# Attention in chunks and a gated feed-forward: another way to bring in v, and another start

## The chip, the cores and the metric

The kernel runs on one core of a Trainium2 chip. The metric is the device time of one execution in microseconds (us). The kernel before took 248.11 us, the median of three runs (247.49 to 249.26).

A core has engines that each work through their own instructions in order and meet at semaphores: TensorE (PE) multiplies matrices, VectorE (DVE) and ScalarE (ACT) do elementwise work, GpSimd (POOL) and SyncE (SP) are used here mostly to issue DMAs (transfers). A tile in SBUF or PSUM has up to 128 partitions, written first in a shape such as 128x512.

## The reference

There are q, k and v of 4 batches, 8 heads, 768 tokens and 64 channels, and 8 memory keys and values for each batch and head. Queries attend in chunks of 32:

```python
for c in range(nc):                      # 24 chunks
    l_start = max(0, 32 * c - 16)        # 16 tokens of left context
    r_end = min(S, 32 * c + 32 + 8)      # 8 tokens of right context
    k_full = np.concatenate([mem_k, k[:, :, l_start:r_end]], axis=2)
    v_full = np.concatenate([mem_v, v[:, :, l_start:r_end]], axis=2)
    scores = scale * np.matmul(q_c, k_full.transpose(0, 1, 3, 2))
    a = softmax(scores)                  # maximum taken off, sum + 1e-9
    out[:, :, c_start:c_end] = np.matmul(a, v_full)
```

The result, as 3072 tokens of 512 channels x, goes through a gated feed-forward with 1536 hidden channels:

```python
gate = np.maximum(x @ w_gate, 0.0)
val = x @ w_val
return (gate * val @ w_out).astype(np.float32)
```

Everything comes and goes as float32. The kernel multiplies in 2-byte types.

## The kernel before, in words

**Tiles.** A tile is 128 tokens of one batch, four chunks, all eight heads: 24 tiles, six for each batch. Each chunk sees 64 keys: 16 left, 32 own, 8 right, 8 memory. The feed-forward works on blocks of 2, 2, 2, 4, 4, 4, 4 and 2 tiles (`BLOCKS`). For each block and each of 12 parts m of 128 hidden channels there are two groups of four matmuls, gate (`g_ps`) and val (`v_ps`, line 396), a relu on ACT (line 402) and a product on DVE (line 408). Then `out_ps` (line 421) is made from w_out, copied by ACT and stored. The gate and val weights come in four groups of parts, 0 to 1, 2 to 5, 6 to 8 and 9 to 11 (`GROUPS`), and the first two blocks take turns by these groups.

**A tile's chain.** The transposes of q and k (`qk_ps`), their copies to `qT` and `kT`, the scores (PE, `s_ps`, line 298), the row maximum (DVE, `mx`, line 311), the difference (DVE, `dif`, line 318), the exponents (ACT, three instructions, line 326, which also reorder the 64 keys to own, right, memory, left), the sum (DVE, line 330), the reciprocal, the product with it (`p_n`, line 341), the transpose (`pT`, line 347), a copy, the values (`xT_ps`), and a copy to `xT`, the feed-forward's input.

**v.** Batches 1 to 3 are loaded into `v_bd`, two tiles of block-diagonal weights. In each, the even heads' 64 key slots lie in partitions 0 to 63 and the odd heads' in partitions 64 to 127; one holds chunks' left, own and right rows (56), then 8 memory rows. Each chunk's 56 rows are read from DRAM (line 173), so that a token that two or three chunks see is read more than once. POOL fills the tile with zeros ahead of its first use (line 129). The values of one tile are then 16 matmuls (line 377). Batch 0 goes another way: v is loaded by tiles of 128 tokens in their natural order (`v_n`, line 188), and PE moves the rows to their chunk slots by multiplying with shifted identities cut from `band` (`vs_ps`, line 204). ACT or DVE copy the result to `v_q`. Its values take 4 matmuls for the memory rows (line 363) and 32 small ones (line 370).

**q and k.** Batch 0 is loaded in pairs of tiles (`qk_p`, line 216), two neighbouring tokens in a partition, and transposed in 8 matmuls for each tile (line 225). The others are loaded tile by tile (`qk_b`, line 243); from tile 18 on SP's DMA transposes them. POOL's loads convert float32 to 2-byte types on the way.

**Order.** Nothing is ordered by hand. `schedule` plays the kernel through with a cost and a priority for each operation and gives every engine the ready operation of the highest priority; the order found is the order in the program, and the engines keep it, whatever the real times are. Loads on POOL keep the order in which they are listed; at most eight are in flight. That list begins with the first k and q pairs, `band`, the second k pair, three `v_n`, weight group 0, the second q pair, the third k pair, two `v_n`, and the weight groups 1 to 3.

Of the kernel before, what the change touches and what calls it, by code (L numbers as in the profile page):

```python
# [9 lines left out]
F32 = mybir.dt.float32  # L10
# [9 lines left out]
def kernel(  # L20
# [20 lines left out]
    CH = 32  # L41
# [11 lines left out]
    BAND0 = 48  # L53

    LATE_QK, LATE_P = 18, 18

# [25 lines left out]

    band = const.tile([128, BAND0 + 176], F16, name="band")
    ident_h = band[:, BAND0:BAND0 + 128]
# [12 lines left out]
    v_q = v_bd[0][:, 0:2].rearrange("p h c d -> p (h c d)").rearrange("p (h c d) -> p h c d", h=HP, d=D)  # L97
    v_n = {}
    qk_p = {(i, r): const.tile([128, H, 2 * D], BF16, name=f"qk_p_{i}_{r}") for i in range(2) for r in range(TPB // 2)}
# [15 lines left out]
    def make_band():  # L115
        nc.gpsimd.memset(band, 0.0)
        nc.gpsimd.affine_select(
            out=band, in_=band, compare_op=ALU.not_equal, fill=1.0, base=BAND0,
            pattern=[[-1, BAND0 + 176]], channel_multiplier=1)

# [7 lines left out]
    def zero(eng, t, hp):  # L128
        eng.memset(t[:, hp].rearrange("p c d -> p (c d)").bitcast(F32), 0.0)  # L129


    def mem_load():
        for par in range(2):
            nc.sync.dma_start(
                kmem_f[:, par, :],
                bass.AP(tensor=mem_k.tensor, offset=mem_k[0, par, 0, 0].offset,
                        ap=[[2 * NMEM * D, B * HP], [D, NMEM], [1, D]]),
            )
# [13 lines left out]
    def mem_rows(eng, b, n):  # L152
        hp, par = divmod(n, 2)
        p = slice(64 * par + CTX, 64 * par + CTX + NMEM)
        src = vmem[p, b, HP * par + hp]
# [22 lines left out]
    def v_parts(b, par, c0, c1):  # L178
        parts = []
        if (b, par, c1) == (B - 1, 1, HP * NCH):  # L180
            c1 -= 1
            parts.append((b, par, 0, 48, c1, c1 + 1))
        return parts + [(b, par, 0, CTX, c0, c1)]


    def load_v_tile(t):
        v_n[t] = ldpool.tile([128, H, D], F16, tag="qk_b", name="v_n")
        nc.gpsimd.dma_start(
            v_n[t],
            bass.AP(tensor=v.tensor, offset=v[0, 0, 128 * t, 0].offset,  # L190
                    ap=[[D, 128], [S * D, H], [1, D]]))

    def shift(c0):
        ps = TMP["sh", c0] = fps.tile([128, 2, HP, D], F32, tag="fps", name="vs_ps")
        for i in range(2):
            t, g = divmod(c0 + i, 4)
            parts = [(t, BAND0 + CH * g - 16)]
            if g == 0 and t:
                parts.append((t - 1, BAND0 + 112))
            if g == 3 and t < TPB - 1:  # L200
                parts.append((t + 1, BAND0 - 48))
            for n, (src, x) in enumerate(parts):
                for par in range(2):
                    nc.tensor.matmul(ps[D * par:D * par + D, i], lhsT=band[:, x:x + 64],  # L204
                                     rhs=v_n[src][:, HP * par:HP * par + HP, :],
                                     start=(n == 0), stop=(n == len(parts) - 1))

    def shift_copy(c0, eng):
        copy(eng, v_q[:, :, c0:c0 + 2, :].rearrange("p h c d -> p c h d"), TMP.pop(("sh", c0)))

# [37 lines left out]
    def new_batch(b):  # L248
        qT[b] = kvpool.tile([128, HP, S], BF16, name="qT")
        kT[b] = kvpool.tile([128, HP, NCH, KW], BF16, name="kT")  # L250
        src = kmemT[:, b]
        nc.vector.tensor_copy(
            kT[b][:, :, :, 16:16 + NMEM],
            bass.AP(tensor=src.tensor, offset=src.offset,
                    ap=[src.ap[0], [NMEM, HP], [0, NCH], [1, NMEM]]))
# [535 lines left out]
```

## Time and profile before

| | before |
|---|---|
| median of three runs | 248.11 us |
| the profiled execution | 247.81 us |
| its span | 246.0 us |
| PE busy | 233.3 us, 95% |
| DVE busy | 132.7 us, 54% |
| ACT busy | 117.6 us, 48% |
| POOL busy, mostly issuing DMAs | 90.6 us, 37% |
| first gate or val matmul | at 22.24 us |

The span is the time from the first to the last instruction that the profiler saw; the execution's own time has 1.8 us around it. Matmuls overlap, so that the time of a group is better read from the start of one group to that of the next. A row of the timeline gives start, duration, engine, line of the kernel, operation, what is written from what, how many instructions are merged, and in brackets how long the engine had been idle and what ended that. In a row of waits, the engine and what waited stand left of the arrow, what it waited for stands right of it.

### The profile page before, as it was taken

Reading aid. Unit: us, or ns where it says so; the run is one execution under the profiler, and the core shown is the slowest. Engines: PE = TensorE matmul, PEld = TensorE weight load, DVE = VectorE, ACT = ScalarE, POOL = GpSimd, SP = SyncE. Lnnn points to the kernel's source line nnn. Section 1 sums busy time; section 2 is a strip of 40 time slices with the busy share of each in tenths; the row PEclk is TensorE's granted clock in tenths of the full one; section 3 lists DMA queues with packets and bytes.
Section 4 is the critical chain, followed back from the end, with each engine's and each line's share of the span. In section 5 each row is a group of like instructions: output and inputs, shape, how many; then the busy total and the mean of one; then the engine's idle time right before and its main releaser. Section 6 shows DMA issues by size and latency. Waiting matters only on the chain.

```text
span 246.0 us, 6397 instructions
## 1 busy us (share of the span) xinstructions
PE 233.3 (95%) x2673; PEld 139.8 (57%) x2673; DVE 132.7 (54%) x260; ACT 117.6 (48%) x265; POOL 90.6 (37%) x105
## 2 busy tenths in 40 slices
PE   0869999999999999999999999999999999999994
PEld 0646887884488645555445545555445444444873
DVE  2372757984139748796048779999342034320430
ACT  2755867753275445643245575765332232312432
POOL 8965799813268991099921050000000000000000
PEclk9999999999999999999999999999999999999999
DMA  7999999999999899999999999671101210002102
GB/s 74 173 179 203 203 96 119 174 175 127 133 223 154 80 102 136 75 75 147 179 192 158 67 76 109 130 147 25 23 0 45 85 44 0 0 35 95 43 3 85
DMA packets 109757, 25.76 MB, mean 105 GB/s; under 512 B 100769, under 2 KB 106657, under 8 KB 109729
## 3 DMA queue, kind: packets, MB, share of 16 engines
q0 software_dynamic: 94368, 16.42, 107.7%
q1 hardware_dynamic: 11760, 2.64, 8.9%
q10 hardware_dynamic: 3600, 6.29, 7.9%
q8 instruction: 21, 0.34, 0.6%
q14 instruction: 8, 0.06, 0.1%
HBM read 32.06 MB, written 6.29 MB: 156 GB/s over the span
## 4 chain that ended last, share of the span: by engine, by line
PE 92%; DMA 2%; DVE 2%; issue 1%; ACT 1%; POOL 1%; ACTq 0%; POOLq 0%
PE v_ps L396 26%; PE g_ps L396 26%; PE out_ps L421 25%; PE xT_ps L377 3%; PE s_ps L298 3%; PE qk_ps L264 2%; DMA qk_p<-in_k_dram 2%; PE pT_ps L347 2%; PE xT_ps L370 2%; PE vs_ps L204 1%; PE qk_ps L225 1%; PE xT_ps L363 1%; DVE mx L311 1%; POOL qk_p L216 1%; DVE dif L318 1%
## 5 line engine op out<-in xcount | busy, mean ns | idle before, releaser
L408 DVE TENSOR_TENSOR gvT<-v_ps,g_relu 128x256 f16<-128x256 f32 (+1 forms) x96 | 53.0, 555 | 56.7 <-PE v_ps L396 41.0
L396 PE MATMUL g_ps<-xT,w_gate_sb 128*128 128x256 f16 (+1 forms) x384 | 78.5, 327 | 0.0
L396 PE MATMUL v_ps<-xT,w_val_sb 128*128 128x256 f16 (+1 forms) x384 | 78.2, 326 | 0.0
L402 ACT ACTIVATE g_relu<-g_ps 128x256 f16<-128x256 f32 (+1 forms) x96 | 46.9, 489 | 50.7 <-PE g_ps L396 50.0
L421 PE MATMUL out_ps<-w_out_sb,gvT 128*128 128x512 f16 (+2 forms) x300 | 65.7, 371 | 0.0
L396 PEld LDWEIGHTS <-w_gate_sb 128*128 128x128 f16 x384 | 36.4, 98 | 24.0 <-issue 0.4
L396 PEld LDWEIGHTS <-w_val_sb 128*128 128x128 f16 x384 | 35.9, 98 | 20.9 <-issue 0.2
L421 PEld LDWEIGHTS <-gvT 128*128 128x128 f16 x300 | 28.0, 98 | 29.9
L78 ACT COPY o_sb<-out_ps 128x512 f32<-128x512 f32 (+2 forms) x25 | 14.2, 567 | 37.2 <-PE out_ps L421 28.2
L326 ACT ACTIVATE p_exp<-dif 128x256 f16<-128x256 f32 (+2 forms) x72 | 19.5, 336 | 9.0 <-DVE dif L318 8.8
L243 POOL DMA_DIRECT2D qk_b<-in_k_dram x18 | 16.5, 915 | 15.0 <-issue 8.4
L311 DVE TENSOR_REDUCE mx<-s_ps 128x8 f32<-128x512 f32 x24 | 16.5, 688 | 8.3 <-PE s_ps L298 8.0
L156 POOL DMA_DIRECT2D v_bd<-vmem x16 | 10.1, 642 | 27.7 <-DMA v_bd<-in_v_dram 27.7
L330 DVE TENSOR_REDUCE sm<-p_exp 128x8 f32<-128x512 f16 x24 | 16.4, 682 | 6.0 <-ACT p_exp L326 5.9
L78 ACT CAST xT<-xT_ps 128x512 f16<-128x512 f32 x19 | 11.1, 584 | 15.4 <-PE xT_ps L377 10.2
L243 POOL DMA_DIRECT2D qk_b<-in_q_dram x18 | 16.4, 913 | 3.1 <-issue 2.0
L341 DVE TENSOR_TENSOR p_n<-p_exp,rinv 128x512 f16<-128x512 f16 x24 | 16.5, 687 | 0.4
L318 DVE TENSOR_TENSOR dif<-s_ps,mx 128x512 f32<-128x512 f32 x24 | 16.4, 684 | 0.4
L173 POOL DMA_DIRECT2D v_bd<-in_v_dram x7 | 14.0, 2015 | 1.0 <-POOL v_bd L129 0.6
L377 PEld LDWEIGHTS <-v_bd 128*128 128x128 f16 x288 | 9.6, 96 | 4.7 <-issue 1.1
L78 ACT COPY kT<-qk_ps 128x512 bf16<-128x512 bf16 x17 | 10.8, 641 | 2.9 <-PE qk_ps L225 1.9
L129 POOL MEMSET v_bd<- 128x1536 f32 x8 | 10.7, 1397 | 0.0
(52 smaller groups left out, 156.8 us busy)
## 6 DMA issues: line engine op xcount, KB each, us to landing
out_dram<-o_sb ACTq DMA_DIRECT2D x23, 256.0 KB
v_bd<-in_v_dram POOLq DMA_DIRECT2D x5, 672.0 KB, 17.6
qk_b<-in_k_dram POOLq DMA_DIRECT2D x18, 128.0 KB, 6.1
qk_b<-in_q_dram POOLq DMA_DIRECT2D x18, 128.0 KB, 6.4
w_out_sb<-in_moe_w_out_dram POOLq DMA_DIRECT2D x2, 768.0 KB, 11.2
qk_p<-in_k_dram POOLq DMA_DIRECT2D x3, 256.0 KB, 5.2
qk_p<-in_q_dram POOLq DMA_DIRECT2D x3, 256.0 KB, 7.1
v_n<-in_v_dram POOLq DMA_DIRECT2D x6, 128.0 KB, 6.5
```

Of the source, the lines that this page charges most:

```text
L78: nc.scalar.copy(o, i)
L243: nc.gpsimd.dma_start(qk_b[a, i], bass.AP(tensor=x.tensor, offset=x[b, 0, 128 * t, 0].offset, ap=[[D, 128], [S * D, H], [1, D]]))
L311: nc.vector.reduce_max(SM[a, "mx"], s4, axis=AX.X)
L318: nc.vector.tensor_tensor(out=SM[a, "dif"].rearrange("p (m r) a s -> p r m a s", r=2), in0=S_ps.pop(a).rearrange("p r (m a) s -> p r m a s ...
L326: nc.scalar.activation(p[:, :, :, s0:s0 + k1 - k0], dif[:, :, :, k0:k1], ACT.Exp, scale=SCALE)
L330: nc.vector.reduce_sum(SM[a, "sm"], SM[a, "p"], axis=AX.X)
L341: nc.vector.tensor_tensor(out=P_n[a], in0=SM.pop((a, "p")), in1=rinv_b, op=ALU.mult)
L377: nc.tensor.matmul(ps[:, hp, r], lhsT=v_bd[b % NSET][:, hp, 4 * t + g, :], rhs=x[:, hp, r], start=True, stop=True)
L396: nc.tensor.matmul(ps, lhsT=w[:, f, 128 * m:128 * m + 128], rhs=xTs[blk][:, f, :], start=(f == 0), stop=(f == NFC - 1))
L402: nc.scalar.activation(st["r", m], st.pop((0, m)), ACT.Relu)
L408: nc.vector.tensor_tensor(out=st["gv"][:, m, :], in0=st.pop((1, m)), in1=st.pop(("r", m)), op=ALU.mult)
L421: nc.tensor.matmul(st["o", t, c], lhsT=st["gv"][:, m, 128 * t:128 * t + 128], rhs=w_out_sb[:, m, c[0]:c[1]], start=(m == 0), stop=(m == ND ...
```

## The change

- **v.** All batches use `v_bd`. Each token is loaded once, into the 32 lower slots of a chunk; these are the 16 left rows and the first 16 own rows, so the chunk grid of the load is shifted by 16 tokens. The other 24 slots of a chunk are copied inside SBUF from the next chunk's lower slots (`upper`, eight copies for each batch on DVE; `upper_tile` for tiles 0 and 1, by ACT or DVE). Batch 0's v is loaded first on POOL, in two halves for even and odd heads. `v_n`, `band`, the shift matmuls and the extra form of the values go. For batch 0 the zeros in `v_bd` are written in 12 pieces by DVE or ACT, and the memory rows are copied by eight DMAs on SP.
- **The first q and k.** Tiles 0 and 1 are loaded as float32 from the queues of SP and ACT into space that is free at the time, converted by DVE or ACT, and transposed in 4 matmuls each. The first eight keys of tiles 1, 2 and 4, which a neighbour's chunk needs, are loaded on their own (`next_load`).
- **Tile 1's exponents** are taken straight from PSUM, one ACT instruction for each head with the negative maximum as bias and the sum as a second result. The reordering of the keys moves to the product with the reciprocal, now three instructions.
- **PE** multiplies zeros (`idle_product`) where the plan has nothing for it up to its 14th us. The plan's costs change with it, and until its 24th us an engine may wait 0.4 us for an operation of higher priority.

In the order that comes out, PE does the first feed-forward group after the values of tiles 0 and 1 and the transposes of the second k pair; ACT has its `upper_tile` copies from v's first half ahead of tile 0's exponents and one from its second half ahead of tile 1's; POOL issues the identity, v's first half, 16 rows, v's second half, weight group 0, the second k and q pairs, group 1, group 2, the third pairs and group 3, with zero fills of the other `v_bd` between them.

```diff
-    band = const.tile([128, BAND0 + 176], F16, name="band")
+    idle = const.tile([128, 128], BF16, name="idle")
+    HEAD = 2
+    DIRECT = (1,)
+    def zero_other(t, par, e):
+        p, c, d = slice(64 * par, 64 * par + 64), slice(4 * t, 4 * t + 4), slice(D - D * par, 2 * D - D * par)
+        x = v_bd[0][p, :, c, d].bitcast(F32)
+        if e == "DVE":
+            nc.vector.memset(x, 0.0)
+            return
...
+    def idle_product(N):
+        if "idle" not in TMP:
+            TMP["idle"] = fps.tile([128, 512], F32, tag="fps", name="idle_ps")
+        nc.tensor.matmul(TMP["idle"][:, 0:N], lhsT=idle, rhs=idle[:, 0:N], start=True, stop=True)
+    def raw_load(eng, x, a, i):
+        src = (q, k)[i]
+        n = 128 if a < HEAD else NMEM
+        eng.dma_start(
+            qk_f[0:n, x],
+            bass.AP(tensor=src.tensor, offset=src[0, 0, 128 * a, 0].offset,
+                    ap=[[D, n], [S * D, H], [1, D]]))
+    def raw_cast(x, a, i, eng):
+        qk_b[a, i] = ldpool.tile([128, H, D], BF16, tag="qk_b", name="qk_b")
+        copy(eng, qk_b[a, i], qk_f[:, x])
-    def load_v_tile(t):
...
-    def shift(c0):
...
+    def upper(b, par, i0, i1, eng):
+        x = v_bd[b % NSET].rearrange("p h c d -> p (h c) d")
+        d = slice(D * par, D * par + D)
+        copy(eng, x[64 * par + CH:64 * par + CTX, i0:i1, d], x[64 * par:64 * par + CTX - CH, i0 + 1:i1 + 1, d])
+    def upper_tile(par, t, eng):
+        d = slice(D * par, D * par + D)
+        copy(eng, v_bd[0][64 * par + CH:64 * par + CTX, :, 4 * t:4 * t + 4, d],
+             v_bd[0][64 * par:64 * par + CTX - CH, :, 4 * t + 1:4 * t + 5, d])
+    def exponent_direct(a):
+        s, nb = S_ps.pop(a), SM.pop((a, "nb"))
+        p = SM[a, "p"] = smpool.tile([128, HP, 2, 64], F16, name="p_exp")
+        SM[a, "sm"] = smpool.tile([128, HP, 2], F32, name="sm")
+        for hp in range(HP):
+            m, r = divmod(hp, 2)
+            for par in range(2):
+                x = 2 * m + par
+                nc.scalar.activation(p[:, hp, par, :], s[:, r, x, :], ACT.Exp, scale=SCALE, bias=nb[:, r, x:x + 1],
+                                     accum_out=SM[a, "sm"][:, hp, par:par + 1])
...
-        if b == 0:
-            for hp in range(HP):
-                nc.tensor.matmul(ps[:, hp, :], lhsT=vmem_0[:, hp, :], rhs=x[:, hp, :],
-                                 start=(hp == 0), stop=False, skip_group_check=True)
...
+    def load_v_op(b, par, deps):
+        n = HP * NCH
+        load(("vl", b, par), CH * n, CH * n * 1.05e-3,
+             lambda: load_v_rows(b, par, 0, CH, 0 if b or par else 1, n), deps)
...
-    load_pair_op(0, 1)
-    load_pair_op(0, 0)
-    load("ident", 0, 0, make_band)
+    load("ident", 0, 0, make_ident)
+    load_v_op(0, 0, [])
+    load_v_op(0, 1, [])
+    load_w_op(0)
     load_pair_op(1, 1)
-    for t in range(3):
-        load_v_nat(t)
-    load_w_op(0)
     load_pair_op(1, 0)
+    load_w_op(1)
+    load_zero(0)
+    load_w_op(2)
...
+                            alone = len(ops[key]["eng"]) == 1 or e == "ACT"
+                            if e != "PE" and t < HASTE and alone and ready(ops[key], t + 0.4):
+                                break
                         if o is None:
+                            if e == "PE" and 1.3 < t < WARM:
+                                order.append((t, lambda: idle_product(128)))
+                                free[e] = t + (0.107 if t < 5.5 else 0.056)
```

## The prediction

> **What bounds the kernel now.** Read the page from the top. The first view gives the busy time of each engine, the second the same in 40 slices of 6.15 us.
>
> ```profile
> span 246.0 us, 6397 instructions
> ...
> PE 233.3 (95%) x2673; PEld 139.8 (57%) x2673; DVE 132.7 (54%) x260; ACT 117.6 (48%) x265; POOL 90.6 (37%) x105
> ...
> PE   0869999999999999999999999999999999999994
> ```
>
> TensorE (PE) is busy 233.3 of 246.0 us and full from the fourth slice to the last but one. Of the 12.7 us idle, 3.15 lie in the last 4 us (results leave; the change does not touch that) and 0.67 at 67 us. The rest, about 9 us, comes before 18.5 us. So two things can move the time: matmuls taken out of the full stretch, and the moment at which the full stretch begins. The timeline shows that moment.
>
> ```profile
> 22.24 1.03 PE L396 MATMUL g_ps<-xT,w_gate_sb 128*128 128x256 f16 x4
> ...
> 23.55 1.36 PE L204 MATMUL vs_ps<-v_n,band 128*64 128x256 f16 x12
> 24.75 0.39 PE L225 MATMUL qk_ps<-ident_b,qk_p 128*64 128x128 bf16 x8
> 25.07 0.61 PE L396 MATMUL v_ps<-xT,w_val_sb 128*128 128x256 f16 x4
> ```
>
> One feed-forward group (four matmuls) runs at 22.24 us, the next only at 25.07; from there they follow each other every 0.43 us (25.07, 25.52, 25.95). The group at 22.24 took 1.03 us, later ones 0.60; twelve shift matmuls took 1.36 us at 23.55 and 0.85 at 26.72. PE runs at about half speed until 24.6 us, though the granted clock reads 1.00 throughout. I count the full stretch from 24.75 us.
>
> **1. PE work, after 24.75 us.** Gone: 34 of the 68 shift matmuls at 0.071 us (twelve in 0.85): 2.4 us. The values of tiles 2 to 5 took 0.93 us each (31.23 to 32.16); the form that replaces them (L377) takes 0.91 for two tiles (67.74 to 68.65): 4 x 0.48 = 1.9. Coming back, because the changed order does it after its first feed-forward group: 16 transposes of the second q pair (37.79 to 38.36, 0.57), the scores of tile 2 (0.31), one group (0.43): 1.3. Net **-3.0**.
>
> **2. When the feed-forward starts.** In the changed order of ACT the two copies that fill tiles 0 and 1 from v's first half stand ahead of tile 0's exponents, and one that needs v's second half stands ahead of tile 1's. ACT works in order, so everything waits for v. On POOL the identity comes first (0.75 us, 3.14 to 3.89 before), then v: its first issue moves from 1.25 to 2.0 us. In this trace the first pair load was issued at 1.25 and had landed at 6.20, the second at 7.66: 1.46 us per load, so 3.5 us pass before data flow; v flows from 5.5 us. Its two halves are 6,128 runs of 64 elements. The nearest rows are the v_n loads (1,024 such runs each, three of them between 9.12 and 12.42 us, so at most 1.1 us per 1,024) and the later v_bd loads (10,752 runs, about 52 to 67.7 us, 1.5 per 1,024). I take 1.3: landed at 9.4 and 13.3 us. The four float32 loads use the same DMA engines; they start 1.3 us sooner, so I charge one of them, 1.0 us: v's second half at **14.3**. Bounds: 12.1 (1.1, nothing beside it) and 20.3 (1.5, all four in the way at 1.46).
>
> From there ACT does: copy 1.05 (from 0.616 for 512 and 0.265 for 128 elements), eight exponents by head 1.5 (the 64-column form takes 0.241 alone, but three forms of 1.01 together run in 0.81; bounds 1.0 to 1.9), copy 1.05, then pT, a zero fill, pT, xT, a zero fill, xT at 0.58 each: 3.5. That is 7.1, and x of both tiles is ready at **21.5**. The first scores do not end later: k, q and the memory keys are issued at 0.74 instead of 1.25, two casts are added (0.58), and even scores at 9.7 as before leave tile 0's exponents ahead of 14.3. PE is full from 21.5 instead of 24.75: **-3.25**. DVE saves dif and sum of tile 1 (0.68 each), beside that wait and so worth nothing; its added fills and copies also fit there.
>
> The idle products (154 matmuls on zeros) cost nothing where PE waits. The 53 ahead of the first pT cover 3.0 us at 56 ns, and then PE waits again until 18 us. Before, PE ran 3.7 us almost without a gap (20.9 to 24.6) before matmuls got short. The Trainium skill (TensorE: Matmul & The Clock Gate, "What's actually happening") says that a window of about 3.4 us without work halves the clock, and as long a busy one restores it. By that rule the first 3.4 us of feed-forward would still be slow and the sum about 1 us higher; the trace agrees on the busy side (3.7 us).
>
> **3. What is late next.** From 21.5 to the values of tile 3, PE has 48 pair transposes (1.7), 18 groups (7.8), two scores (0.6), two pT (0.6), two values (0.9): 11.6 us. Before, scores 2 to values 3 took 13.2 us (23.21 to 36.4), of which 3.3 lay between the two scores; the new order has one group there (0.75 with the scores). So 10.7, and 2.7 ahead of scores 2: 13.4. PE idles the difference, **+1.8**. Weights: POOL's issues at the end of the queue were released at 23.06, 24.38, 25.64, so 1.3 us per 512-column load. Behind v: group 0 (2.6) 16.9, two pairs 19.8, group 1 24.9, group 2 28.7, two pairs 31.6, group 3 35.4. Needed from about 25 and 29.5: just in time. They stand behind v in one queue and move with it.
>
> **4. Batches 1 to 3.** v's runs fall from 56 to 32 rows per chunk, which removes the 0.67 us at 67 us:
>
> ```profile
> 67.74 1.06 PE L377 MATMUL xT_ps<-pT,v_bd 128*128 128x32 f16 x32 [0.67 <-PE out_ps L421]
> 68.03 0.58 ACT L78 COPY o_sb<-out_ps 128x512 f32<-128x512 f32 x1 [2.93 <-DMA out_dram<-o_sb]
> 68.07 0.88 POOL L243 DMA_DIRECT2D qk_b<-in_k_dram  x1 [5.28 <-DMA v_bd<-in_v_dram]
> ```
>
> POOL's DMA there ended with v, as did PE's wait. Added: 24 DVE copies of 24x1536. The nearest row is the copy of 768 two-byte elements inside SBUF, 0.31 at its best, so 0.62: 15 us on an engine that is 46% idle, in rows of four (2.5 us) ahead of reductions. I put 0.2 us a row for six rows: 1.2. Net **+0.5**. The other end is the same copy beside a v issue:
>
> ```profile
> 84.22 4.40 POOL L173 DMA_DIRECT2D v_bd<-in_v_dram  x2 [0.57 <-POOL v_bd L129]
> ...
> 84.69 1.90 DVE L252 COPY kT<-kmemT 128x768 bf16<-128x768 bf16 x1
> ```
>
> It took 1.90 us, ending as the first issue did. Beside a shorter issue at 37.44 it took 0.35. The Trainium skill (SBUF — State Buffer, "Who interferes with whom") says that such a DVE copy and GpSimd exclude each other for a whole instruction, the later one waiting. By that rule each row of four waits for an issue in progress; what it would cost is rival E.
>
> **Sum.** 246.0 - 3.0 - 3.25 + 1.8 + 0.5 = 242.05 us of span. The profiled execution took 247.81, 1.8 more than its span: **243.9 us**. Against the median of 248.11 that is 1.7% less; 1% (245.6 to 250.6) is about what this kernel's measurement can tell. Every microsecond by which v's second half misses 14.3 counts one to one, since exponents and weights stand behind it.
>
> **Rivals.** A, the forecast, 242 to 246, chance 0.38.
> B, v at its best rate (12.1) and the chain of tiles 2 and 3 hidden: 246 - 3.0 - 5.45 + 0.5 + 1.8 = 239.9. For it: the v_n rows are the nearest in time. Against: eight loads share the DMA engines. 0.20.
> C, the gain of the start is given back: x of tile 3 comes at 36.4 as before, DVE having five fills and eight copies ahead of tile 2's maximum, and PE still slow (+1.2). 246 - 3.0 + 0.5 + 1.2 + 1.8 = 246.5. For it: 4 us of added DVE work there. Against: before, DVE idled 4.56 us ahead of that maximum. 0.16.
> D, slower: v arrives late. It lands in 32 partitions at a time, not 128 as v_n nor 56 as v_bd; if the rate goes with that, 1.5 x 56/32 = 2.6 us per 1,024, its second half lands at 5.5 + 15.6 + 1.0 = 22.1 and the time is 251.7. It loses from 18.5 us on. For it: 56-row loads were slower than 128-row ones. Against: the v_bd rows run beside stores. 0.18.
> E, the DVE copies are held by POOL's issues: if each of the six rows waits 0.9 us (one qk_b issue) and PE with it, 243.9 + 5.4 = 249.3; each copy at 1.90 would be far more. 0.08.
>
> **The numbers.** Faster by over 1% (below 245.6): 0.35 of A, B, 0.03 of C: 0.58. Within 1%: 0.03 + 0.12 + 0.02 of D + 0.05 of E: 0.22. Slower: 0.01 of C, 0.16 of D, 0.03 of E: 0.20. The range goes from B's 239.9 to 250.7, short of D's upper part.
>
> **What would show it.** ACT's copy from v's second half near 14.3 us; the first g_ps near 21.5 and short; PE idle about 2 us before tile 3's values; no vs_ps; v_bd copies on DVE near 0.6 us; no wait near 62 us. A copy at 18 us or later makes the forecast wrong, and so do copies of 1 to 2 us.

## The result and the profile after

The changed kernel took **259.88 us** (median, 259.27 to 260.29) beside 248.45 us (247.49 to 249.26) of the kernel before: 1.046 times the time, 95% interval 1.041 to 1.051. It is 11.4 us slower; 243.9 was forecast, and 259.88 lies outside the range as well. The profiled execution took 259.27 us, its span is 257.4 us: 11.4 more than the span before. The ratios here and below leave out executions that took over 1.5% more than the shortest of their kernel; only for a_early does this change much.

The head of the page of the changed kernel, the busy times and the 40 slices of PE (now 6.4 us each) with its granted clock:

```profile
span 257.4 us, 6412 instructions
...
PE 236.0 (92%) x2627; PEld 143.4 (56%) x2627; DVE 155.8 (61%) x309; ACT 121.4 (47%) x278; POOL 81.2 (32%) x103
...
PE   5982588999969999899999999999999999999994
...
PEclk9997599999999999999999999999999999999999
```

The 154 idle products make up 13.6 us of PE's 236.0 (their group on the page). What is left, 222.4, is 10.9 less than the 233.3 of before: the matmuls did go away. Apart from the second slice, which idle products help to fill, the slices read 9 only from the eighth on (45 us), with a 6 from 71 to 77 us and an 8 from 103 to 109. The timeline of PE in the changed kernel (start, duration, engine and line, operation, then in brackets how long PE had waited and for what):

```profile
12.36 0.32 PE L324 MATMUL s_ps<-kT,qT 64*32 64x48 bf16 x32
...
16.25 0.31 PE L324 MATMUL s_ps<-kT,qT 64*32 64x64 bf16 x32
...
23.20 0.39 PE L412 MATMUL xT_ps<-pT,v_bd 128*128 128x32 f16 x8 [0.39 <-ACT v_bd L140]
26.48 0.38 PE L412 MATMUL xT_ps<-pT,v_bd 128*128 128x32 f16 x8 [2.89 <-DMA v_bd<-vmem]
...
28.09 0.51 PE L412 MATMUL xT_ps<-pT,v_bd 128*128 128x32 f16 x12 [1.23 <-DVE v_bd L137]
...
30.47 1.03 PE L431 MATMUL g_ps<-xT,w_gate_sb 128*128 128x256 f16 x4
```

The scores of the same tiles in the kernel before:

```profile
9.71 0.41 PE L298 MATMUL s_ps<-kT,qT 64*32 64x48 bf16 x32
...
11.95 0.54 PE L298 MATMUL s_ps<-kT,qT 64*32 64x64 bf16 x32 [0.20 <-DVE dif L318]
```

The scores of tiles 0 and 1 come at 12.36 and 16.25 (before: 9.71 and 11.95). Of tile 0's values twelve matmuls run by 23.20, the last four wait for a transfer until 26.48, and the first feed-forward group runs at 30.47 instead of 22.24. That splits the loss in two. The engines from the first group to the end of the span, before and after (stretch, length, busy time and instructions of PE, PEld, DVE, ACT and POOL, then the granted clock, DMA share, GB/s):

```profile
22.24:246.00 223.76, 219.94 (x2436) 130.15 (x2434) 123.77 (x241) 105.61 (x243) 73.11 (x77) 1.00 1.23 100
```

```profile
30.47:257.40 226.93, 217.32 (x2334) 126.84 (x2332) 141.18 (x271) 105.01 (x240) 59.25 (x71) 0.99 0.77 85
```

| | before | after | difference |
|---|---|---|---|
| start of the first feed-forward group | 22.24 | 30.47 | +8.23 |
| from there to the end of the span | 223.76 | 226.93 | +3.17 |
| of it PE busy | 219.94 | 217.32 | -2.62 |
| of it PE idle | 3.82 | 9.61 | +5.79 |

So nearly three quarters of the loss lie ahead of the first group, in which ACT stands at the middle. ACT's timeline in the changed kernel, only the rows at which its chain turns:

```profile
13.80 0.62 ACT L79 CAST qk_b<-v_bd 128x512 bf16<-128x512 f32 x1 [2.24 <-DMA v_bd<-in_k_dram]
14.44 1.99 ACT L79 COPY v_bd<-v_bd 24x1024 f16<-24x1024 f16 x2
...
18.36 0.31 ACT L367 ACTIVATE p_exp<-s_ps,nb 128x64 f16<-128x64 f32 x1
18.57 0.19 ACT L367 ACTIVATION_READ_ACCUMULATOR p_exp<-s_ps,nb 128x1 f32 x1
...
20.86 1.04 ACT L79 COPY v_bd<-v_bd 24x1024 f16<-24x1024 f16 x1
```

ACT waits for **tile 1's k**, the first row: it lands at 13.8. The copies from v stand behind that cast in ACT's order, not in wait for v. The loads show why k was late. The timeline of POOL, and then of SP, in the changed kernel:

```profile
1.52 3.33 POOL L218 DMA_DIRECT2D v_bd<-in_v_dram  x3 [0.22 <-issue]
...
10.20 0.88 POOL L238 DMA_DIRECT2D qk_p<-in_q_dram  x1 [1.98 <-DMA v_bd<-in_v_dram]
...
14.64 0.62 POOL L110 DMA_DIRECT2D w_gate_sb<-in_moe_w_gate_dram  x1 [2.92 <-DMA v_bd<-in_v_dram]
```

```profile
5.34 0.62 SPq L210 DMA_DIRECT2D v_bd<-in_mem_v_dram  x2
6.01 0.40 SPq L164 DMA_DIRECT2D v_bd<-in_k_dram  x1
11.33 6.66 SPq L201 DMA_DIRECT2D v_bd<-vmem  x8
```

POOL's waits end as v's halves land, at 10.2 and 14.6, close to the 9.4 and 14.3 of the sum. Tile 1's k, though, is issued on SP only at 6.01 (five other loads and the two of the memory values stand ahead) and flies for 7.8 us. Order is not all of it: SP stands for 1.8 us ahead of the memory values, and the waits put this down to tile 0's q, loaded on ACT's queue.

```profile
SPq L210 <- DMA v_bd<-in_q_dram: 1.8, 1, 1.8
```

No run tested this wait. The eight transfers of the memory rows start at 11.33, once the memory values have landed (10.9) and been converted, and the last of them ends PE's wait at 26.48.

From 50 us on, the slot copies on DVE show, here in front of a reduction of batch 1 (timeline of the changed kernel, DVE, POOL and PE):

```profile
70.81 3.73 DVE L81 COPY v_bd<-v_bd 24x1536 f16<-24x1536 f16 x4
...
70.93 3.72 POOL L218 DMA_DIRECT2D v_bd<-in_v_dram  x4
...
75.32 0.40 PE L395 MATMUL pT_ps<-ident_h,p_n 128*128 128x128 f16 x4 [2.32 <-DVE p_n L384]
```

### The profile page after: what moved, and what is told of

The parts are those of the page before. It is cut to its first block, busy times and chain, and to the rows that moved or that the text cites. A ratio compares the mean times of both kernels' runs of the same rounds, so it can differ in the third digit from the quotient of the medians.

```text
span 257.4 us, 6412 instructions
## 1 busy us (share of the span) xinstructions
PE 236.0 (92%) x2627; PEld 143.4 (56%) x2627; DVE 155.8 (61%) x309; ACT 121.4 (47%) x278; POOL 81.2 (32%) x103
## 4 chain that ended last, share of the span: by engine, by line
PE 75%; DVE 10%; DMA 7%; SPq 2%; ACT 2%; issue 2%; ACTq 0%; DVEq 0%
PE g_ps L431 23%; PE v_ps L431 22%; PE out_ps L456 21%; DVE v_bd L81 4%; DMA v_bd<-vmem 4%; PE xT_ps L412 4%; SPq L201 2%; DMA v_bd<-in_mem_v_dram 2%; PE qk_ps L290 2%; DMA v_bd<-in_q_dram 2%; PE pT_ps L395 2%; PE s_ps L324 2%; DVE gvT L443 1%; DVE mx L337 1%; DVE sm L372 1%
## 5 line engine op out<-in xcount | busy, mean ns | idle before, releaser
L352 ACT ACTIVATE p_exp<-dif 128x256 f16<-128x256 f32 (+2 forms) x69 | 18.7, 334 | 15.5 <-DVE dif L344 15.3
L81 DVE COPY v_bd<-v_bd 24x1536 f16<-24x1536 f16 (+3 forms) x32 | 20.5, 682 | 0.4
L218 POOL DMA_DIRECT2D v_bd<-in_v_dram x17 | 15.9, 956 | 10.4 <-DMA w_out_sb<-in_moe_w_out_dram 5.2
L412 PE MATMUL xT_ps<-pT,v_bd 128*128 128x32 f16 x384 | 13.6, 177 | 5.0 <-DMA v_bd<-vmem 2.9
L412 PEld LDWEIGHTS <-v_bd 128*128 128x128 f16 x384 | 13.1, 96 | 8.9 <-issue 3.6
L372 DVE TENSOR_REDUCE sm<-p_exp 128x8 f32<-128x512 f16 x23 | 15.6, 680 | 1.9 <-ACT p_exp L352 1.7
L384 DVE TENSOR_TENSOR p_n<-p_exp,rinv 128x512 f16<-128x512 f16 x23 | 15.8, 688 | 0.5
L344 DVE TENSOR_TENSOR dif<-s_ps,mx 128x512 f32<-128x512 f32 x23 | 15.7, 681 | 0.2
L150 PE MATMUL idle_ps<-idle 128*128 128x128 bf16 x154 | 13.6, 257 | 1.0 <-DVE idle L495 1.0
L79 ACT CAST xT<-xT_ps 128x512 f16<-128x512 f32 x18 | 10.5, 581 | 7.6 <-PE xT_ps L412 6.7
## 6 DMA issues: line engine op xcount, KB each, us to landing
w_out_sb<-in_moe_w_out_dram POOLq DMA_DIRECT2D x2, 768.0 KB, 10.2
```

The source lines that it names most:

```text
L79: nc.scalar.copy(o, i)
L81: eng.tensor_copy(o, i)
L218: nc.gpsimd.dma_start(dst[64 * par + s0:64 * par + s1, c0:c1, D * par:D * par + D], bass.AP(tensor=v.tensor, offset=v[b, HP * par, 0, 0].o ...
L352: nc.scalar.activation(p[:, :, :, s0:s0 + k1 - k0], dif[:, :, :, k0:k1], ACT.Exp, scale=SCALE)
L372: nc.vector.reduce_sum(SM[a, "sm"], SM[a, "p"], axis=AX.X)
L412: nc.tensor.matmul(ps[:, hp, r], lhsT=v_bd[b % NSET][:, hp, 4 * t + g, :], rhs=x[:, hp, r], start=True, stop=True)
```

## The experiments

The time lost against the kernel before, by ratio (so many per cent of 248.45 us), and the start of the first feed-forward group in the profiled execution. "after" and "before" name the two kernels.

| run | ratio, 95% interval | lost, us | first group |
|---|---|---|---|
| after | 1.046 (1.041 to 1.051) | 11.4 | 30.47 |
| a_zeros | 1.036 (1.028 to 1.044) | 8.9 | 29.89 |
| a_rows | 1.035 (1.026 to 1.044) | 8.7 | 31.15 |
| a_both | 1.034 (1.027 to 1.042) | 8.5 | 33.50 |
| a_pe | 1.046 (1.040 to 1.052) | 11.5 | 26.68 |
| a_warm | 1.050 (1.047 to 1.054) | 12.4 | 31.87 |
| a_nodirect | 1.050 (1.045 to 1.054) | 12.3 | 35.62 |
| a_early | 1.018 (1.014 to 1.022) | 4.4 | 27.89 |
| b_q | 1.028 (1.022 to 1.033) | 6.9 | 31.48 |
| b_q_early | 1.022 (1.017 to 1.026) | 5.3 | 31.27 |
| quiet (one execution) | 255.14 us beside 248.03 | 7.1 | 22.78 |
| b_late | 1.007 (1.005 to 1.010) | 1.8 | 21.53 |
| v_alone | 1.021 (1.017 to 1.024) | 5.1 | 25.81 |
| v_first_batch | 1.015 (1.011 to 1.018) | 3.6 | 25.85 |
| v_alone_2 | 1.004 (1.001 to 1.007) | 1.0 | 25.21 |
| v_first_2 | 1.000 (0.998 to 1.003) | 0.1 | 23.92 |
| v_pe | 1.019 (1.014 to 1.023) | 4.6 | 27.52 |
| v_mend | 1.013 (1.009 to 1.017) | 3.3 | 24.41 |
| v_mend_2 | 1.034 (1.029 to 1.039) | 8.4 | 24.14 |

### What holds the first values: zero fills or memory rows

The first theory took the wait ahead of the values of tile 0 as the whole loss: either the zero fills that take turns with them, or the memory rows' transfers. Three edits of the changed kernel: all fills ahead of the first values; the rows by four copies on DVE instead of eight transfers; both.

```diff
 a_zeros
-  + [("z0", t, par) for par in range(2) if b == 0]
+  + [("z0", x, par) for x in range(TPB) for par in range(2) if b == 0]
 a_rows
-    for n in range(2 * HP):
-        op(("mr", 0, n), {"SP": 0.72}, lambda e, n=n: mem_rows(nc.sync, 0, n), ["vm0"], (0, 0))
+    for n, (c0, c1) in enumerate(((0, 8), (0, 8), (8, NCH), (8, NCH))):
+        op(("mr", 0, n), {"DVE": ...}, lambda e, ...: rows_copy(n % 2, c0, c1), ["vm0"], ...)
```

> The changed kernel, but every zero fill of batch 0's v_bd stands ahead of the first values. In the changed kernel's trace the first values of tile 0 run at 26.48 us, when the last DMA of memory rows has landed, then fills and values take turns (1.23 and 1.26 us of waiting), and the first gate group runs at 30.47 us. Theory 1 (the DMAs of memory rows set the start): values of tile 0 stay at 26.4, the turns go, the first gate group comes at 29.0 and the time falls by 1 to 1.5 us, to about 258.6. Theory 2 (the fills are what holds the values): first gate near 25, time near 255.

> The changed kernel, but batch 0's memory rows are written by four DVE copies in place of eight DMAs. Theory 1: values of tile 0 follow pT's copy, at 23 to 24 us in place of 26.48, the first gate group at about 27, time lower by 3 to 4 us, near 256.3. Theory 2: no more than 1 us is gained, since the values still wait for fills. Third theory (the late k pair of tile 1 and its scores set the start by themselves): values not before 25.

> Both edits: memory rows by DVE copies, all fills ahead of the values. Theories 1 and 2 together: no wait for DMA or fills is left, first gate group near 25 us, time 5 us lower, near 255. Still slower than the kernel before, by what comes after 46 us (about 3 us) and by tile 1's late scores (16.25 us). If the start were the whole loss, 249.

All three kept at least 8.5 of the 11.4 us, and their intervals overlap with that of "after". In a_zeros the turn-taking is gone and the values still wait for the rows, until 27.1; the first group came 0.6 us earlier. In a_rows the rows' wait is gone and two others take its place. Its timeline, DVE, PE and ACT:

```profile
11.30 3.91 DVE L210 COPY v_bd<-vmem 32x2048 f16<-32x2048 f16 x4
...
14.68 5.42 PE L150 MATMUL idle_ps<-idle 128*128 128x128 bf16 x65
...
15.48 0.58 ACT L79 COPY kT<-qk_ps 128x512 bf16<-128x512 bf16 x1
...
20.03 0.31 PE L331 MATMUL s_ps<-kT,qT 64*32 64x64 bf16 x32
```

The four copies stand ahead of tile 0's maximum. Tile 1's scores came at 20.03 instead of 16.25, though its kT was copied by 16.1: ahead of them PE worked through 65 idle products, which keep their place in its order however late the rest is. The first values came at 26.38. In a_both the same 65 hold the scores until 20.87. So these two runs do not show the rows' wait by itself; as the whole loss, the first theory fell.

### The first batch without the rows' wait, a warm clock, no direct exponents

a_pe adds the memory values of the first batch by four matmuls per tile, as the kernel before did, and moves the fills of tiles 2 to 5 behind tile 1's values. a_warm adds 104 idle products where PE waits. a_nodirect takes tile 1's exponents back to the common form.

```diff
 a_pe
+        if b == 0:
+            for hp in range(HP):
+                nc.tensor.matmul(ps[:, hp, :], lhsT=vmem_0[:, hp, :], rhs=x[:, hp, :], start=(hp == 0), stop=False, ...)
 a_warm
-  lambda e, a=a: p_t(a)
+  lambda e, a=a: (idle_more(32 if a == 1 else 0), p_t(a))
...
-  lambda e, a=a: values(a),
+  lambda e, a=a: (idle_more(72 if a == 0 else 0), values(a)),
 a_nodirect
-    DIRECT = (1,)
+    DIRECT = ()
```

> The changed kernel, but batch 0's memory rows are multiplied by TensorE as before the change (four matmuls more for a tile, zeros in their place in v_bd), so that no DMA of memory rows is waited for and DVE gets no copies in their place; fills of tiles 2 to 5 come behind the values of tile 1. Theories 1 and 2 (rows' DMAs and fills set the start): values of tile 0 follow pT's copy at 22.6 to 23, the first gate group comes near 25.5 in place of 30.47; PE gets 24 matmuls more, some 1.6 us after that; time about 256. Theory 5 (DVE and ACT, which do the casts, fills and copies one after the other, set the start): first gate not before 28.

> The changed kernel with 104 products on zeros more, 32 ahead of pT of tile 1 and 72 ahead of the values of tile 0, in the 5 us in which PE waits. Theory 3 (the granted clock fell to 0.50 because PE idled from 20 to 28 us, and the first 3 us of the feed-forward pay for it): granted clock near 1 in this stretch, the first gate group 0.60 in place of 1.03, time 1 to 1.5 us lower, near 258.6. Rival: the groups up to 34 us wait for weights and copies anyway, time within 0.5.

> The changed kernel with tile 1's exponents as before the change (difference on DVE, three ACT instructions, sum on DVE). By the traces the eight exponents with their sums take 2.47 us of ACT against 0.81, ahead of both pT copies. If ACT's order sets the start: values of tile 0 near 26.4 all the same, since the rows' DMAs land then, and the time within 1 us of the changed kernel's 259.9. If the direct form saves what DVE had to do: 1 us slower.

In a_pe the first group came 3.8 us earlier and ran in 0.61 instead of 1.03 us; then scores 2 waited 3.00 us for a qT copy that stood on DVE behind two fills of 1.76 us and smaller ones, and the time did not move. Here the gain at the start was given back on DVE (and PE has 24 matmuls more). For the clock, the stretches of "after" and of a_warm (length, busy time and instructions of PE, PEld, DVE, ACT, POOL, then the granted clock, DMA share, GB/s):

```profile
20.00:25.00 5.00, 1.18 (x19) 0.72 (x16) 1.52 (x5) 3.55 (x10) 2.55 (x4) 0.77 1.36 204
25.00:30.00 5.00, 1.55 (x31) 1.30 (x33) 2.04 (x5) 1.94 (x4) 5.00 (x8) 0.50 1.48 195
30.00:35.00 5.00, 5.00 (x76) 3.02 (x75) 4.76 (x10) 3.31 (x6) 3.74 (x5) 0.71 1.40 184
```

```profile
25.00:30.00 5.00, 3.76 (x85) 3.66 (x83) 0.97 (x2) 0.59 (x1) 4.95 (x8) 1.00 1.46 190
30.00:35.00 5.00, 4.04 (x91) 2.82 (x88) 4.38 (x10) 4.32 (x8) 4.00 (x6) 1.00 1.43 189
```

Where PE of "after" ran 1.2 and 1.6 us in five, the clock fell to 0.50; a_warm read 1.00 from 20 us on. The time did not fall, but that does not settle what the clock costs. In a_warm's profiled execution the first gate group took 0.61 us instead of 1.03, and from its start to that of the third 1.77 us passed instead of 2.85; but the 72 products stand ahead of tile 0's values until 27.86 (26.48 in "after"), and the first group came 1.4 us later. So one microsecond won stands against one lost. The clock also fell in a_warm, earlier: 0.66 from 15 to 20 us, behind a wait of 3.33 us for tile 1's k. Nor do the direct exponents show in the time: a_nodirect lies within 1 us of "after" (its profiled execution was its longest, 262.64 us, hence the late first group in the table).

### The order of the small loads

a_early issues the memory values early on SP instead of behind the neighbours' keys, and tile 1's k ahead of the neighbours' keys. It also moves the fills of tiles 2 to 5 behind tile 1's values, as a_pe does.

```diff
-  prio=((-12, -12, -7, -10)[x],))
+  prio=((-12, -12, -8.5, -10)[x],))
-  op("vml", {"SP": 0.8}, lambda e: pattern_load(), ["vmem_f"], prio=(-7.5,))
+  op("vml", {"SP": 0.8}, lambda e: pattern_load(), ["vmem_f"], prio=(-11.5,))
...
-  after=["warm2", "vmem_f"])
+  after=["warm2", "vmem_f"] + ([("v", HEAD - 1)] if t >= HEAD else []))
```

> The changed kernel with another order of the small loads: the memory values as SP's second load, tile 1's k ahead of the three loads of neighbours' keys; fills of tiles 2 to 5 behind the values of tile 1. Theory 6 (loads are late because each waits for one of the earlier ones to end, 4.7 us): memory values in by 6 to 7 in place of 10.7 us, tile 1's k by 7 in place of 13.8, its scores near 13 in place of 16.25, the rows' DMAs landed by 18, the first gate near 23.5, time near 253. Theory 7 (loads on these queues are late because they share the DMA engines with v and the weights): rows land no earlier than 22, first gate 27 or later, time 257 or more.

This was the first edit with a clear gain: 4.4 us lost instead of 11.4. Its four executions took 252.2, 252.4, 256.1 and 257.5 us; the ratio goes by the two shorter ones, and by the median of all four the loss is 6.4 us. Even the longest lies under the shortest of "after" (259.27). The memory values land at 6.0, and no values wait for rows any more. Tile 1's k, in the timeline of SP and DVE:

```profile
2.97 0.59 SPq L164 DMA_DIRECT2D v_bd<-in_k_dram  x1
...
10.45 0.43 DVE L81 CAST qk_b<-v_bd 128x512 bf16<-128x512 f32 x1 [1.91 <-DMA v_bd<-in_k_dram]
```

It lands at 10.4, still after a flight of 7.5 us. The first scores came later than in "after" all the same (14.56 and 16.86), since the neighbours' keys, now issued behind it at 5.4 to 6.4, are cast at 12.0 and transposed at 13.57: what was moved ahead pushed the others back. How much of the gain is the order of the loads and how much the place of the fills, this run does not separate; a_zeros, which moved the fills the other way, changed the time by less than its interval can tell. (The profiled execution is one of the two longer ones, 256.05 us; only its order of events is read.)

### The q/k start by itself, and who slows it

b_q keeps v of all batches as before and takes only the new start: float32 q and k by SP and ACT, idle products, direct exponents. b_q_early has the load order of a_early. quiet holds POOL's loads back until tile 1's k has landed, by a small POOL copy out of it.

```diff
 quiet, against b_q
+        if t == 0:
+            quiet = const.tile([128, 8], F32, name="quiet")
+            nc.gpsimd.tensor_copy(quiet, qk_f[:, 2, 0, 0:8])
-  load(("vn", t), 1024, 1.05, lambda: load_v_tile(t), take=["qk"])
+  load(("vn", t), 1024, 1.05, lambda: load_v_tile(t), [("raw", 1, 1)], take=["qk"])
```

> v of all batches as in the kernel before; of the change only the first q and k as float32 by the queues of SP and ACT, the products on zeros and tile 1's exponents by head. If this part of the change gains (scores of tiles 0 and 1 earlier, v_n loads at the head of POOL's queue): first gate near 20 in place of 22.24 and the full stretch near 22.5 in place of 24.75, time near 246. Rival (loads on these queues are slow beside POOL's, as in the changed kernel, where tile 1's k landed at 13.8): first gate at 22 to 24, time 248 to 250.

> v as before the change, q and k's start as changed, but POOL issues no load before tile 1's k has landed (one POOL copy that reads it stands ahead of the first load). The kernel gets slower by that; what is wanted are the small loads. Theory 7 (they are late because they share the DMA engines with POOL's loads): tile 0's k and q land by 3.5, tile 1's k is issued by 4.5 and lands 2 to 3 us later, by 7. Theory 6 (each waits for one of the earlier ones): they still take 5 to 9 us from issue to landing, tile 1's k lands after 11.

> As the run with v of all batches as before and the new start of q and k (255.5), but the memory values are SP's second load and tile 1's k stands ahead of the three loads of neighbours' keys. There tile 1's k was issued at 5.98 and landed at 15.7, its scores came at 19.5, the first gate at 31.5. Theory 6 (the order and the waits of small loads for earlier ones are the cause): tile 1's k lands by 10, scores of both tiles by 14, first gate near 24, time near 249.5. Theory 7 (any ten small loads beside POOL's stream take until 12 to 14): the neighbours' keys are now the late ones, scores of tile 0 at 14, first gate 25 to 27, time 251 to 253.

The start alone loses 6.9 us, with v's loads as they were. Its k and what follows, from the timeline of b_q (SP, ACT, PE), and then the same of quiet:

```profile
5.98 0.81 SPq L154 DMA_DIRECT2D v_bd<-in_k_dram  x1
...
15.75 0.62 ACT L80 CAST qk_b<-v_bd 128x512 bf16<-128x512 f32 x1 [3.49 <-DMA v_bd<-in_k_dram]
...
19.49 0.41 PE L337 MATMUL s_ps<-kT,qT 64*32 64x64 bf16 x32
```

```profile
6.05 0.40 SPq L154 DMA_DIRECT2D v_bd<-in_k_dram  x1
...
9.08 0.19 POOL L224 COPY quiet<-v_bd 128x8 f32<-128x8 f32 x1 [7.62 <-DMA v_bd<-in_k_dram]
...
13.53 0.31 PE L340 MATMUL s_ps<-kT,qT 64*32 64x64 bf16 x32
```

The same load, issued at the same moment, flies 9.8 us beside POOL's loads and 3.0 us without them. The first group comes 8.7 us earlier (22.78 instead of 31.48), about where it was before the change; some 2.6 of these are scores, shift matmuls and transposes that b_q has ahead of that group (28.86 to 31.48) and quiet behind it. The time does not fall: POOL's loads (v, pairs and weights) now start at 9.2, so that held apart, the loads only change places. The order alone (b_q_early) brings 1.5 us, and its interval overlaps with that of b_q. Even in quiet, k is issued only at 6.05, with the same wait of SP (1.9 us) ahead of the memory values: the second part of the delay is the place in SP's line.

The Trainium skill (DMA: Bandwidth & Descriptors, "Issuing engines are not separate DMA queues") says that DMAs started from any engine run on the same 16 DMA engines and interleave, and that another issuing engine saves only the time of issue. The pair b_q and quiet agrees: 9.8 against 3.0 us.

### Batches 1 to 3 by themselves

b_late is the kernel before with v once per token in batches 1 to 3 only.

```diff
+    for b in range(1, B):
+        for n in range(2 * HP):
...
+            op(("up", b, n), {"DVE": ...}, lambda e, ...: upper(b, par, i0, i1, engine[e]), [("vl", b, par)], (1, TPB * b - 1, 12))
```

> The kernel before with one part of the change: v of batches 1 to 3 once per token, the other slots by 24 DVE copies; batch 0 and q and k as before. Theory 4 (rows of four copies hold DVE 3 to 3.7 us, longer beside POOL's issues, and PE waits for p_n): 2 to 4 us slower than before, about 251.5, with a PE wait of 2 us or more near 73 us. The prediction's step 4: 0.5 us slower, near 249.

It loses 1.8 us (1.3 to 2.4); +0.5 was forecast for this part. PE idles 1.93 us between 50 and 100 us where it idled 0.67 before, and more after that, in rows such as this one of its timeline:

```profile
99.06 0.40 PE L344 MATMUL pT_ps<-band,p_n 128*128 128x128 f16 x4 [1.24 <-DVE p_n L338]
```

The copies' mean is 0.72 us (18 of 24x1536), against 0.62 in the sum, but between 0.54 and 1.05.

### The v part by itself

v_alone is the changed kernel with the q/k start of the kernel before. In it the third k pair stands behind weight group 2, as in the changed kernel; but without the loads of the neighbours' keys tile 3's scores need it. v_alone_2 moves it ahead of group 1, as before. v_first_2 is the same with batches 1 to 3 as before.

```diff
 v_alone_2, against v_alone
     load_pair_op(1, 0)
+    load_pair_op(2, 1)
     load_w_op(1)
...
-    load_pair_op(2, 1)
     load_pair_op(2, 0)
```

> One part of the change alone: v once per token in chunk slots in all four batches; the first q and k by POOL in pairs, ahead of v, the exponents and PE's order without products on zeros, as before the change. Theory 8 (the loss is the new start of q and k: with it alone and v as before, the first gate came at 31.48 and the time was 255.5): scores of tiles 0 and 1 near 9.7 and 12 as before, v's halves land near 13.5 and 18, first gate near 23, the time within 247 to 250, with 1.8 of it from the copies of batches 1 to 3. Theories 1 and 2 (v in batch 0 costs most, by its rows' DMAs, fills and copies): first gate at 27 or later, time 253 or more.

> As the run with the v part alone, but batches 1 to 3 load v as before the change (56 rows for each chunk, no copies on DVE). Step 1 and 2 of the prediction for v alone: 4.3 us of PE work less (2.4 for shifts, 1.9 for values), first gate near 23, so 3 us less than before if v is in time, about 245; if v in batch 0 costs what it saves, 248. Against the run with v in all batches: 1.8 less by the earlier run, 0.5 by the prediction's step 4.

> As the run with the v part alone (253.1), but the third k pair is loaded ahead of weight group 1, as before the change. In that run it stood behind group 2; tile 3's scores, which need it without the extra loads of neighbours' keys, came at 37.1, 9.2 us after tile 2's (3.3 before the change), and PE idled 3 us between 35 and 50. If that order was an artefact of the run and cost what PE idled: tile 3's scores by 32, time 3 us lower, near 250. If PE would have waited for DVE in any case: within 1 us of 253.

> v by the changed way in the first batch only, batches 1 to 3 as before, q and k by POOL's pair loads with the third k pair ahead of the second group's weights as before. Theory 8 (the first batch's v part is by itself a small gain, since it takes about 9 us of matmuls out of PE, and what v_alone_2 lost came from the slot copies of batches 1 to 3, 1.8 us in b_late): 250.05 - 1.8 = 248.2, within 0.5 of the kernel before, idle time of PE between 50 and 100 us below 1. Rival (the first batch's own waits, 2 to 3 us for the memory rows' transfers and for the reductions held by slot copies, give more back than the matmuls bring): 249.5 or more, idle below 1 between 50 and 100 but over 19 us before 50. Second rival (copies and rows overlap with the pair loads and the gain is whole): 246.5.

v_alone lost 5.1 us, but mostly by that k pair: scores 3 followed scores 2 after 9.2 us (27.96, 37.11). With the pair in its old place they follow after 2.0, and the loss is 1.0 us. An earlier run, v_first_batch, had the pair in the late place too, and lost 3.6; in it one load for the last batch's last chunk goes into the neighbouring chunk, so that the last chunk has old rows. In v_first_2 the difference is gone: 0.1 us, interval -0.6 to +0.8. PE's waits in v_alone_2 (in total, times, longest):

```profile
PE pT_ps L368 <- DVE p_n L357: 5.9, 4, 2.1
...
PE xT_ps L385 <- DMA v_bd<-vmem: 3.0, 2, 2.0
```

and in v_first_2:

```profile
PE pT_ps L368 <- DVE p_n L357: 3.7, 2, 2.1
PE xT_ps L385 <- ACT v_bd L79: 2.2, 1, 2.2
PE xT_ps L385 <- DMA v_bd<-vmem: 2.0, 1, 2.0
```

The first batch's v costs nothing and brings nothing: in the profiled execution the first group comes 1.7 us later (23.92), and from there the span is 3.4 us shorter (220.38): PE is busy 4.8 less (215.18 against 219.94) and idle 1.4 more. That execution, at 246.1 us the shortest of twelve, is 2.4 below the median, so these two numbers stand for the direction only.

### Three attempts to mend the first batch

v_pe adds the memory values by matmuls (as in a_pe) to the first batch's v alone. v_mend copies the slots in six pieces behind tile 1's product and puts POOL's fills behind the weights. v_mend_2 has in addition the k pair early and DVE's own zeros behind that product.

```diff
 v_mend
+    for t0 in (2, 4):
+        for par in range(2):
+            op(("up", t0, par), {"DVE": 0.8}, lambda e, ...: upper_tiles(par, t0), ..., after=[("nrm", 1)])
...
-    load_zero(0)
...
+    for hp in range(HP):
+        load_zero(hp)
```

> As the run in which only the first batch's v goes the new way (251.65), but the memory rows are multiplied by TensorE as before the change (24 matmuls more, about 2 us of PE), so that no DMA of rows is waited for. There the values of tile 0 ended at 22.0 behind a row DMA and the first gate came at 25.85. Theory 1 (the rows' DMAs cost the v part its start): values of tile 0 near 18, first gate near 23.3, time 2.5 lower for the start and some 1.5 higher for the added matmuls, near 250.6. Theory 4 (DVE's slot copies hold tile 1's sum, 6 us for 4 copies beside POOL's fills): first gate still at 25 or later, time 251.5 to 253.

> As the run before it, and in addition the slot copies of tiles 2 to 5 stand behind tile 1's product and are 4 larger ones (and 2 small) in place of 8, and POOL's four fills of the other v_bd come after all weights. Theory 4: tile 1's sum follows its exponents at once, first gate near 21.5, PE nearly full from 23 on, and the 4.3 us of PE work that the prediction's step 1 takes out show, less 2 for the rows: time 244.5 to 246.5, under the kernel before. Rival (weights and v come too late in POOL's queue, whatever DVE does): 249 or more, with PE waits on weights or q's copies between 25 and 45 us.

> As the run v_mend (251.8: first batch's v the new way, memory rows by TensorE, slot copies behind tile 1's product, POOL's fills behind the weights), with the third k pair ahead of weight group 1 and the zeros of tiles 2 to 5 behind tile 1's product, so that tile 0's scores come at 9.7 in place of 11.25. If v in chunk slots is worth what step 1 of the prediction counted once nothing is in its way: first gate near 22.5, tile 3's scores by 29, PE without gaps from 23 us on, time 245 to 247. If the work that it puts on DVE and POOL's queue (fills, copies, v ahead of weights) takes the place of each wait taken away: 248 or more.

None of the three comes down to the kernel before. In v_pe slot copies stand ahead of tile 1's sum (3.93 us for three of 24x1024), and PE waits 4.7 us. v_pe and v_mend still have the late k pair (scores 3 at 39.62 and 36.43). v_mend_2 shows best what DVE's copies meet. Its timeline, DVE, POOL and PE:

```profile
29.83 5.35 POOL L128 MEMSET v_bd<- 128x1536 f32 x4
...
29.99 5.92 DVE L81 COPY v_bd<-v_bd 24x1792 f16<-24x1792 f16 x2
...
36.69 0.41 PE L299 MATMUL s_ps<-kT,qT 64*32 64x64 bf16 x32 [6.98 <-DVE dif L319]
```

The longest copy of this row took 5.67 us, another of the same shape behind dif 0.62. The row ends just after POOL's four memsets, tile 2's dif comes behind it, and PE stands for 7 us. The Trainium skill (SBUF — State Buffer, "Who interferes with whom") says that such a copy and GpSimd shut each other out for a whole instruction. The trace agrees that they do, but the copy lasted through four memsets of 1.34 us, not one.

No version was faster than the kernel before; v_first_2 equals it.

## Why the prediction was wrong

**The step that failed** is in step 2: "The first scores do not end later: k, q and the memory keys are issued at 0.74 instead of 1.25". Only the first load of each queue was issued at 0.74 (the memory keys, at 0.74 before, moved to 1.27). Tile 1's k, issued at 6.0, landed at 13.8, and its scores came 4.3 us later than before (0.9 of it behind idle products, since kT was copied by 15.4). I had charged v with the company of the float32 loads (1.0 us), but not the float32 loads with that of v. b_q shows that this start loses 6.9 of the 11.4 us without any change to v; quiet shows that the flight is three times as long beside POOL's loads, and the trace of a_early that the order on SP decides what is late. That the late k makes up the whole 6.9 is argued: quiet brings k early, but its time pays for POOL's later loads instead.

**A transfer was left out of the chain.** My row "pT, a zero fill, pT, xT, a zero fill, xT" had the fills and not the eight memory-row transfers, which the new form of the values needs in the first batch, where the kernel before had matmuls. Against the sum's 21.5 (its own terms add up to 21.4), x of both tiles was ready at 29.85, 8.35 later. At the copy behind the exponents ACT is 4.0 late (done at 21.9 instead of 17.9): 1.0 by the exponents, 3.0 by tile 1's k, whose cast holds ACT's order until 14.4: from there the copies and tile 0's exponents follow one another until 18.3. The other 4.35 arise behind that, where PE waits 2.89 for the rows and 1.23 for a fill. The row transfers start late because the memory values land at 10.9, and that is again the line of small loads. The parts alone lose 6.9 (b_q) and 1.0 (v_alone_2), 7.9 in sum; some 3.5 arise only where both meet, and a_early, which moves two of the small loads and the fills, takes 5 to 7 away. That v's loads at the head of POOL's queue slow the small ones is how I read it; no run held v back in the changed kernel itself.

**v's landing was right**, 10.2 and 14.6 against 9.4 and 14.3, and so rival D was false: the loss came by a load that had no rival of its own.

**The exponents** took 2.47 us instead of 1.5, above the bound of 1.9: each head issues a second instruction of 0.19 to 0.24 us that reads the sum. As a_nodirect shows, this had no measurable price.

**The idle products and the clock**: the rule cited there, a slow clock after a wait, came true (0.50, first groups of 1.03 us, against 0.61 at a reading of 1.00 in a_warm). What the microsecond that I named for it is worth, no run shows: the products with which a_warm removed it also stood ahead of the values. That they "cost nothing where PE waits" holds only while the plan's times hold. Behind late loads the products stood ahead of work that was ready: of tile 1's scores by 0.9 us in the changed kernel, where ACT was busy until 18.3 anyway, and by up to 4 us in a_rows and a_both. No run left them out of the changed kernel.

**Step 1 came out about right**: PE's time from the first group on fell by 2.62 in the changed kernel, -3.0 in the sum, though the first groups ran slowly in both (1.03 us).

**Step 3** was close: tile 3's values came at 45.7, and PE idled 2.2 us between the first group and them, where +1.8 had been put. Rival C's reason, DVE's fills and copies ahead of tile 2's maximum, is real: they run from 26.9 to 34.4, and a_pe and v_mend_2 show what they cost when the start comes earlier.

**Step 4 was mis-sized**: +1.8 in b_late instead of +0.5. Rival E's mechanism fits the trace, though no run took POOL's issues away from the copies. In the changed kernel PE waits 2.3 us at 75.32 behind four copies that ended with POOL's v issues, and idles 2.35 between 50 and 100 us and 1.23 between 100 and 150, against 0.67 and 0: 2.9 more. E's price of 5.4 was too high.

## What to carry to other kernels

A load moved to another issuing engine is to be priced by its landing: its place in that engine's line, and the flight beside everything else that flies then; here the first put the issue 5 us later, and the second made a flight of 9.8 us out of 3.0. Where a matmul is replaced by a transfer or by copies on DVE, put these into the chain ahead of its reader, and look for POOL's instructions in the same microseconds. And a change of several parts is best run part by part with the order of the other loads kept, since one k pair in another place cost more (4 us) than the part under test.

## What the runs showed of the hardware that I had not expected

- A load of 256 KB issued on SP at 6 us took 3.0 us with no loads on POOL's queue and 9.8 us beside POOL's loads (quiet, b_q).
- A DVE copy of 24x1792 two-byte elements, 0.62 us where it ran freely, took 5.67 us beside four POOL memsets in a row (v_mend_2); four of 24x1536 took 3.73 beside four POOL issues of 3.72.
- An exponent by head with a sum is two instructions on ACT, 0.30 to 0.35 and 0.19 to 0.24 us; eight took 2.47 us.
- The granted clock fell from 1.00 to 0.50 within 10 us in which PE worked 2.7 us, and 104 products on zeros, which kept it at 1.00 there, gave no shorter time; they stood ahead of the values themselves.
